# First batch's choice of an expert in single slots, early rows loaded in front of the early weights, first expert's rows loaded in two parts

## The chip, the core and the metric

The kernel runs on one core of a Trainium2 chip. The metric is the device time of one execution in microseconds (us). A core has TensorE (matrix products; PE in the profile), VectorE (DVE), ScalarE (ACT), GpSimd (POOL) and SyncE (SP, which here issues nearly all DMAs), each with an instruction queue of its own that it works through in order.

## The reference

Three stages: clustered attention, a layer of eight experts with one expert for each token, and a dense layer with a gate. 1536 tokens (2 batches of 768), 8 heads of 64, 512 channels.

```
mask   = q_assign == k_assign                      # cluster of each query and key: argmax over 16 centroids
attn   = softmax(where(mask, q k^T / 8, -1e9)) v   # per batch and head, 768 x 768
x      = attn as (1536, 512)
e_idx  = argmax(x w_gate); gate = softmax(x w_gate)[e_idx]; eom = sigmoid(x w_output_gate)[e_idx]
out[t] = gate * eom * relu(x[t] w1[e_idx]) w2[e_idx]          # w1 (8, 512, 1024), w2 (8, 1024, 512)
h      = out w_in;  result = (h * sigmoid(1.702 h)) w_out     # w_in (512, 2048), w_out (2048, 512), both 64-bit floats
```

## The kernel before

**Attention.** A unit is a batch and a pair of heads (8 units); a step is one head and 128 queries of a unit (96 steps, `steps`). In step i of the loop at L939 TensorE makes the scores of step i+1 (`emit_scores`), VectorE takes their maximum (L518), TensorE transposes the probabilities of step i-1 in two halves (`emit_pt`), the first of which ScalarE copies out (L537) and the second VectorE (L539), and ScalarE takes the exponential of step i+1 (L524). Products with v (L567) and with the output weights (L586) come in between, the latter into the only bank of the pool `ps_m`. The next unit's operands are prepared at fixed steps (`PLAN`): transposes, the split into high and low parts on GpSimd (L343, L344), stacks by DMA (L362), and the choice of clusters on VectorE (L391 to L405). Pieces of a conversion of the dense layer's 64-bit weights (`convert_early`, L125 to L135, written out at L176) run at fixed steps (`slots`).

**Routing.** As soon as a batch's attention, or half of the second batch's, is done, `route(gi)` chooses the experts of its tokens on VectorE (small instructions of 8 to 48 elements in each partition), counts, finds each token's row, scales the tokens, and scatters them to `xd` in memory (GpSimd, L730). It is a generator: `advance(2)` at L540 runs two pieces, from one `yield` to the next, after each half of a step's transposes, so a step has four slots. `route(0)` is put in at step 61. Its rank sums (L652 to L661) lie in a bank of `ps_m` that VectorE reads until L691. In the middle it picks the expert with the most tokens in the first batch (`soonh`, `soon`), and up to 128 of that expert's tokens (the early rows), which are computed during the rest of attention.

**Early rows.** `soon_at` sets the steps: at 75 `soon_ids` reads the expert and its row into registers of SyncE; at 84 seven loads of that expert's weights are issued, at 87 five more, and behind them the early rows (`soon_rows`, which waits for all scatters of the first batch); at 91 `soon_x` transposes the rows (L790). The products (`soon_products`, L806 and L816) run while the other groups are routed.

**Branch and experts.** Each expert has a capacity (`CAPS`, 304 for the first); if some expert has more tokens, a loop of surplus tiles runs inside `tc.If(trips > 0)` (L1233), which with these inputs is passed over. Every engine reads `trip` (L1228) and branches. Before that point two halves of the first expert's weights are loaded and split (`loads_to(2)`). Behind it `win_start(0, True)` loads the first expert's 304 rows in three pieces of 128, 128 and 48, each after all twelve scatters of L730; `loads_to(6)` loads four more halves of weights; `win_x` transposes the rows (L1118) and splits them (L1122, L1123); then the loop over 64 half blocks (L1337) and the dense layer (L1385 on) follow. Instructions are issued in the order in which they are written (`tc.manual_schedule`).

The lines on which the steps of the prediction rest:

```
921: soon_at = {75: [soon_ids], 84: [lambda: next(weights)], 87: [lambda: next(weights), soon_rows], 91: [soon_x]}
539:     nc.vector.tensor_copy(dst, src)
540: advance(2)
1102: for r0 in range(0, nr, 1 if pieces else nr):
1103:     m, p = (1, min(128, n - r0 * 128)) if pieces else (nr, 128)
```

Of the kernel before, what the change touches and what calls it, by code (L numbers as in the profile page):

```python
# [9 lines left out]
F32 = mybir.dt.float32  # L10
# [36 lines left out]
def attention_moe_ffn(ctx: ExitStack, tc: tile.TileContext, q, k, v, centroids, w_gate, w_og, w1, w2, w_in, w_out, out):  # L47
# [3 lines left out]
    def f32(ap):  # L51
        return ap.bitcast(F32)
# [553 lines left out]
    def route(gi):  # L606
# [62 lines left out]
        if gi == 0:  # L669
            nc.vector.scalar_tensor_tensor(lk, part, float(E), rev8, op0=ALU.mult, op1=ALU.add)  # L670
            lm, lv = new("lm", [128, 1]), new("lv", [128, E])
            nc.vector.tensor_reduce(lm, lk, op=ALU.max, axis=AX.X)
            nc.vector.tensor_scalar(soonh, lk, lm, None, op0=ALU.is_equal)
            yield
            nc.vector.tensor_tensor(lv, soonh, part, op=ALU.mult)
            nc.vector.tensor_reduce(ngone, lv, op=ALU.add, axis=AX.X)
            nc.vector.tensor_scalar(ngone, ngone, float(FIRST), None, op0=ALU.min)
            yield
            nc.vector.tensor_scalar(gone, soonh, ngone, None, op0=ALU.mult)
            nc.vector.scalar_tensor_tensor(sbase, gone, -1.0, ebase, op0=ALU.mult, op1=ALU.add)  # L680
            nc.vector.scalar_tensor_tensor(srev8, gone, -float(E), rev8, op0=ALU.mult, op1=ALU.add)
            yield
            nc.vector.tensor_tensor(lv, soonh, ebase, op=ALU.mult)
            nc.vector.tensor_reduce(span[:, 1:2], lv, op=ALU.add, axis=AX.X)
            nc.vector.tensor_tensor(span[:, 0:1], span[:, 1:2], ngone, op=ALU.subtract)
            yield
            nc.vector.tensor_tensor(lv, soonh, iota8, op=ALU.mult)
            nc.vector.tensor_reduce(lm, lv, op=ALU.add, axis=AX.X)
            nc.vector.tensor_copy(soon[:, 0:1], lm[0:1])
            nc.vector.tensor_copy(soon[:, 1:2], span[0:1, 0:1])  # L690
        nc.vector.tensor_tensor(dest, rk, sbase[:, None, :].to_broadcast([128, nj, E]), op=ALU.add)  # L691
# [229 lines left out]
    soon_at = {75: [soon_ids], 84: [lambda: next(weights)], 87: [lambda: next(weights), soon_rows], 91: [soon_x]}  # L921
# [173 lines left out]
    def win_load(ex_row, n, one_tile=False, pieces=False):  # L1095
        nr = -(-n // 128)
        if one_tile:
            x = hp.tile([128, 2 * CAP], F32R, name="ht", tag="ht")[:, None, :DM].bitcast(F32)
        else:
            x = xp.tile([128, WR, DM], F32, name="xr", tag="xr", bufs=1)  # L1100
        d = {"n": n, "nr": nr, "x": x}
        for r0 in range(0, nr, 1 if pieces else nr):
            m, p = (1, min(128, n - r0 * 128)) if pieces else (nr, 128)
            row = nc.s_assert_within(ex_row + r0 * 128, 0, E * NT - 128, skip_runtime_bounds_check_because="inside the rows of an expert") if r0 else ex_row
            x = nc.sync.dma_start(out=d["x"][:p, r0:r0 + m], in_=xd[bass.ds(row + FIRST, m * p)].rearrange("(r p) c -> p r c", p=p)).ins
            need(x, scatters)
        return d

    def win_x(d, r):
# [4 lines left out]
        m = min(128, d["n"] - r * 128)  # L1114
# [5 lines left out]
        hi = d["t"][:, :, n + r * 128:n + r * 128 + m]  # L1120
        src = pt.rearrange("p (k n) -> p k n", k=4)[:, :, :m]
        nc.scalar.copy(hi, src)  # L1122
        nc.vector.tensor_tensor(d["t"][:, :, r * 128:r * 128 + m], src, f32(hi), op=ALU.subtract)  # L1123
# [86 lines left out]
    hp = cx.enter_context(tc.tile_pool(name="hp", reuse_waits="tile", bufs=3))  # L1210

# [13 lines left out]
    some(100)  # L1225
    for f in low_parts:
        f()
# [94 lines left out]
    with tc.manual_schedule():  # L1322
        win_start(0, True)
# [169 lines left out]
```

## Time and profile before

| | us |
|---|---|
| median of 3 runs | 731.31 |
| lowest and highest | 730.92, 732.39 |
| profiled execution, its own time | 733.72 |
| span of the profiled execution | 732.0 |

| engine | busy us | share of the span |
|---|---|---|
| TensorE, products | 703.2 | 96% |
| VectorE | 458.1 | 63% |
| ScalarE | 393.0 | 54% |
| GpSimd | 264.4 | 36% |

A timeline has one line for each run of equal instructions of an engine: start, duration, engine, line of the kernel, operation, the tile written and those read, shapes, count, and in brackets how long the engine idled before it and who ended that. "issue" means that the engine waited for nothing that the profile shows; a name with q is an engine's sequencer. The table of stretches gives for each stretch its length, the busy time of each engine with its count of instructions, the mean granted clock of TensorE (1.00 is 2.4 GHz, 0.50 is 1.2 GHz), and the busy share and rate of the DMA engines. Attention takes the first 270 us, the branch lies near 280 us, the experts end near 460 us, and the dense layer takes the rest.

### The profile page before, as it was taken

To read this page: it belongs to the slowest core of one execution; us is meant where nothing else is said; L and a number is where in the kernel's file an instruction comes from. 1 tells how busy PE (TensorE), PEld (TensorE's weight loads), DVE (VectorE), ACT (ScalarE), POOL (GpSimd) and SP (SyncE) were. 2 spreads that over 40 slices of the span, in tenths; PEclk is the share of its full clock that TensorE was granted. 3 is DMA by queue.
4 is the path that set the end of the run, shared out by engine and by line. 5 is a ranking of instruction groups with operands and counts; after the bars stand their busy time and mean duration, and the time that the engine had idled before them with its cause. 6 is when DMAs were issued, how large, how long until landed. Compare 5 with 4: busy or idle time off the path is not lost.

```text
span 732.0 us, 12543 instructions
## 1 busy us (share of the span) xinstructions
PE 703.2 (96%) x4522; PEld 580.2 (79%) x4522; DVE 458.1 (63%) x886; ACT 393.0 (54%) x789; POOL 264.4 (36%) x219
## 2 busy tenths in 40 slices
PE   8999999998999898999999897999999999999996
PEld 6776776776866678999999887888888888888885
DVE  6969788889888774344554545687655657232322
ACT  7767675675666544556777676544534344222120
POOL 2230330312750013755978889222432212020202
PEclk8999999999899999999999999999999999999999
DMA  6778969637274427766477776132643211010101
GB/s 195 171 189 266 238 216 293 142 121 173 69 200 141 174 86 255 230 215 215 161 254 243 236 224 222 59 116 86 68 73 41 81 59 56 1 58 1 58 0 58
DMA packets 70594, 105.18 MB, mean 144 GB/s; under 512 B 9648, under 2 KB 48304, under 8 KB 70528
## 3 DMA queue, kind: packets, MB, share of 16 engines
q1 hardware_dynamic: 67584, 95.94, 45.9%
q0 software_dynamic: 2944, 8.40, 3.0%
q8 instruction: 37, 0.61, 0.4%
q14 instruction: 29, 0.24, 0.1%
HBM read 70.46 MB, written 14.69 MB: 116 GB/s over the span
## 4 chain that ended last, share of the span: by engine, by line
PE 33%; issue 16%; ACT 5%; DVE 3%; POOL 2%; DMA 1%; POOLq 0%; ACTq 0%; DVEq 0%
PE ph L1317 4%; PE ph L1318 4%; PE ph L1319 4%; PE py L1412 3%; PE py L1411 3%; PE py L1410 3%; PE py L1134 3%; ACT w L1048 3%; PE ph L1134 3%; PE ph L1135 1%; PE py L1135 1%; DVE w L1051 1%; DMA raw<-in_moe_w_dram 1%; POOL out_dram L1421 1%; ACT hs L1140 1%
## 5 line engine op out<-in xcount | busy, mean ns | idle before, releaser
L1051 POOL TENSOR_TENSOR w<-raw,w 128x1024 fp32r<-128x1024 f32 x51 | 125.6, 2482 | 39.3 <-ACT w L1048 38.9
L518 DVE TENSOR_REDUCE nm<-sp 128x1 f32<-128x768 f32 x96 | 91.6, 955 | 16.2 <-PE sp L516 14.1
L1395 DVE TENSOR_TENSOR sg<-ph,sg 128x512 f32<-128x512 f32 x48 | 33.2, 691 | 99.7 <-ACT sg L1394 97.5
L524 ACT ACTIVATE P<-sp,nm 128x768 f32<-128x768 f32 x96 | 87.2, 908 | 11.3 <-DVE nm L518 10.6
L532 PEld LDWEIGHTS pt<-ident,P 128*128 128x128 f32 x576 | 66.4, 143 | 28.1 <-issue 17.5
L532 PE MATMUL pt<-ident,P 128*128 128x128 f32 x576 | 84.3, 280 | 4.0 <-ACT pT L537 2.1
L1394 ACT ACTIVATE sg<-ph 128x512 f32<-128x512 f32 x48 | 28.7, 597 | 104.7 <-PE ph L1319 100.3
L1134 PE MATMUL py<-ht,w 128*128 128x512 f32 (+6 forms) x224 | 70.2, 367 | 8.0 <-DVE ht L1158 5.1
L515 PE MATMUL sp<-X,Q 128*128 128x384 f32 x192 | 74.9, 390 | 0.5 <-ACT P L524 0.4
L1412 PE MATMUL py<-w,gl 128*128 128x512 f32 (+1 forms) x194 | 75.2, 387 | 0.0
L1411 PE MATMUL py<-w,gh 128*128 128x512 f32 (+1 forms) x194 | 75.1, 387 | 0.0
L1410 PE MATMUL py<-w,gh 128*128 128x512 f32 (+1 forms) x194 | 75.0, 387 | 0.0
L1317 PE MATMUL ph<-yth,w 128*128 128x512 f32 x192 | 74.8, 390 | 0.0
L1318 PE MATMUL ph<-ytl,w 128*128 128x512 f32 x192 | 74.7, 389 | 0.0
L1319 PE MATMUL ph<-yth,w 128*128 128x512 f32 x192 | 74.7, 389 | 0.0
L1084 POOL TENSOR_TENSOR w<-csq,w 128x512 fp32r<-128x512 f32 x24 | 32.7, 1364 | 115.7 <-ACT w L1083 115.7
L1048 ACT CAST w<-raw 128x1024 fp32r<-128x1024 f32 x68 | 70.5, 1042 | 4.2 <-issue 2.4
L1134 PE MATMUL ph<-t,w 128*128 128x512 f32 (+6 forms) x224 | 69.4, 365 | 0.4 <-DVE ht L1158 0.4
L567 PE MATMUL po<-pT,ld_v 128*32 128x384 f32 x768 | 69.0, 492 | 0.0
L516 PE MATMUL sp<-Z,Q 80*128 80x384 f32 x192 | 66.4, 346 | 0.5 <-DMA Q<-ohT 0.5
L537 ACT COPY pT<-pt 128x384 f32<-128x384 f32 x96 | 45.8, 477 | 36.8 <-PE pt L532 36.8
L539 DVE COPY pT<-pt 128x384 f32<-128x384 f32 x96 | 52.8, 550 | 12.6 <-PE pt L532 12.2
(291 smaller groups left out, 1476.2 us busy)
## 6 DMA issues: line engine op xcount, KB each, us to landing
raw<-in_moe_w_dram SPq DMA_DIRECT2D x64, 512.0 KB, 4.5
raw<-in_moe_w_in_dram SPq DMA_DIRECT2D x16, 512.0 KB, 4.1
raw<-in_moe_w_out_dram SPq DMA_DIRECT2D x16, 512.0 KB, 4.8
xd<-zrow SPq DMA_DIRECT2D x8, 768.0 KB, 5.9
Q<-Hq SPq DMA_DIRECT2D x28, 192.0 KB, 2.7
ew<-in_moe_w_dram SPq DMA_DIRECT2D x9, 384.0 KB, 7.8
ld_q<-in_q_dram SPq DMA_DIRECT2D x8, 384.0 KB, 6.0
ld_k<-in_k_dram SPq DMA_DIRECT2D x8, 384.0 KB, 3.8
```

The costliest lines, as they stand in the source:

```text
L518: nc.vector.tensor_reduce(nm, sp[:, :, :384], op=ALU.max, axis=AX.XY, negate=True)
L524: nc.scalar.activation(P, L["sp"][:, :, :384], AF.Exp, bias=L["nm"], accum_out=L["sm"][:, h, j % 3:j % 3 + 1])
L532: nc.tensor.transpose(pt[:, r * 128:(r + 1) * 128], L["P"][:, n, r * 128:(r + 1) * 128], ident)
L1048: nc.scalar.copy(hi, r)
L1051: (eng or nc.gpsimd).tensor_tensor(lo, r, f32(hi), op=ALU.subtract)
L1134: nc.tensor.matmul(ps[:, :2 * n], w_hi, t, start=first, stop=False)
L1317: nc.tensor.matmul(ph, wa(key, 0, k, i), yth[:, k, cs], start=(k == 0), stop=False)
L1318: nc.tensor.matmul(ph, wa(key, 0, k, i), ytl[:, k, cs], start=False, stop=False)
L1319: nc.tensor.matmul(ph, wa(key, 1, k, i), yth[:, k, cs], start=False, stop=(k == 3))
L1410: nc.tensor.matmul(po[m][:, cs], gh[:, ms], wb(key, 0, i)[:, cs], start=first, stop=False)
L1411: nc.tensor.matmul(po[m][:, cs], gh[:, ms], wb(key, 1, i)[:, cs], start=False, stop=False)
L1412: nc.tensor.matmul(po[m][:, cs], gl[:, ms], wb(key, 0, i)[:, cs], start=False, stop=last)
```

## The change

1. In `route(0)`, the first batch's choice gets a `yield` after nearly every instruction. `dest` is started in the first slot from the rank sums and `ebase`, and `part` is copied to `c0`, so the bank isn't read after that; at the end of the choice `gone` is subtracted from `dest`.
2. In `soon_at`, `soon_rows` is called at step 84 in front of the first seven weight loads, and `soon_ids` at step 78.
3. `win_start(0, True)` is called in front of the reading of `trip` and the branch, and there loads only the first 128 rows, after the scatters of the first two groups; the last three scatters are declared to be without a dependency on it. Behind the branch `rest` loads the other 176 rows in one DMA of 88 partitions with two rows each, after all scatters. `win_x` then works on pieces of 128, 88 and 88 rows. The tile `xr` moves to a pool of its own, `xrp`, behind the pool `hp`.

```
--- before.py
+++ after.py
@@ -667,28 +667,44 @@
         if gi < len(GROUPS) - 1:
             lk = new("lk", [128, E])
         if gi == 0:
-            nc.vector.scalar_tensor_tensor(lk, part, float(E), rev8, op0=ALU.mult, op1=ALU.add)
-            lm, lv = new("lm", [128, 1]), new("lv", [128, E])
+            nc.vector.tensor_tensor(dest, rk, ebase[:, None, :].to_broadcast([128, nj, E]), op=ALU.add)
+            lm, lv, c0 = new("lm", [128, 1]), new("lv", [128, E]), new("c0", [128, E])
+            nc.vector.tensor_copy(c0, part)
+            yield
+            nc.vector.scalar_tensor_tensor(lk, c0, float(E), rev8, op0=ALU.mult, op1=ALU.add)
+            yield
             nc.vector.tensor_reduce(lm, lk, op=ALU.max, axis=AX.X)
+            yield
             nc.vector.tensor_scalar(soonh, lk, lm, None, op0=ALU.is_equal)
             yield
-            nc.vector.tensor_tensor(lv, soonh, part, op=ALU.mult)
+            nc.vector.tensor_tensor(lv, soonh, c0, op=ALU.mult)
+            yield
             nc.vector.tensor_reduce(ngone, lv, op=ALU.add, axis=AX.X)
+            yield
             nc.vector.tensor_scalar(ngone, ngone, float(FIRST), None, op0=ALU.min)
             yield
             nc.vector.tensor_scalar(gone, soonh, ngone, None, op0=ALU.mult)
+            yield
             nc.vector.scalar_tensor_tensor(sbase, gone, -1.0, ebase, op0=ALU.mult, op1=ALU.add)
+            yield
             nc.vector.scalar_tensor_tensor(srev8, gone, -float(E), rev8, op0=ALU.mult, op1=ALU.add)
             yield
             nc.vector.tensor_tensor(lv, soonh, ebase, op=ALU.mult)
+            yield
             nc.vector.tensor_reduce(span[:, 1:2], lv, op=ALU.add, axis=AX.X)
+            yield
             nc.vector.tensor_tensor(span[:, 0:1], span[:, 1:2], ngone, op=ALU.subtract)
             yield
+            nc.vector.tensor_copy(soon[:, 1:2], span[0:1, 0:1])
             nc.vector.tensor_tensor(lv, soonh, iota8, op=ALU.mult)
+            yield
             nc.vector.tensor_reduce(lm, lv, op=ALU.add, axis=AX.X)
+            yield
             nc.vector.tensor_copy(soon[:, 0:1], lm[0:1])
-            nc.vector.tensor_copy(soon[:, 1:2], span[0:1, 0:1])
-        nc.vector.tensor_tensor(dest, rk, sbase[:, None, :].to_broadcast([128, nj, E]), op=ALU.add)
+            yield
+            nc.vector.tensor_tensor(dest, dest, gone[:, None, :].to_broadcast([128, nj, E]), op=ALU.subtract)
+        else:
+            nc.vector.tensor_tensor(dest, rk, sbase[:, None, :].to_broadcast([128, nj, E]), op=ALU.add)
         if gi == len(GROUPS) - 2:
             nc.vector.scalar_tensor_tensor(lk, part, float(E), srev8, op0=ALU.mult, op1=ALU.add)
         yield
@@ -918,7 +934,7 @@
     slots.update({21: 3, 27: 1, 75: 1, 80: 1, 81: 2, 86: 3, 87: 2, 92: 2, 93: 2})
 
     weights = soon_weights()
-    soon_at = {75: [soon_ids], 84: [lambda: next(weights)], 87: [lambda: next(weights), soon_rows], 91: [soon_x]}
+    soon_at = {78: [soon_ids], 84: [soon_rows, lambda: next(weights)], 87: [lambda: next(weights)], 91: [soon_x]}
 
     fixed = ExitStack()
     fixed.enter_context(tc.manual_schedule())
@@ -1097,13 +1113,25 @@
         if one_tile:
             x = hp.tile([128, 2 * CAP], F32R, name="ht", tag="ht")[:, None, :DM].bitcast(F32)
         else:
-            x = xp.tile([128, WR, DM], F32, name="xr", tag="xr", bufs=1)
-        d = {"n": n, "nr": nr, "x": x}
-        for r0 in range(0, nr, 1 if pieces else nr):
-            m, p = (1, min(128, n - r0 * 128)) if pieces else (nr, 128)
+            x = xrp.tile([128, WR, DM], F32, name="xr", tag="xr")
+        d = {"n": n, "nr": nr, "x": x, "rows": [128] * (nr - 1) + [n - 128 * (nr - 1)]}
+
+        def rows_of(r0, m, p, names):
             row = nc.s_assert_within(ex_row + r0 * 128, 0, E * NT - 128, skip_runtime_bounds_check_because="inside the rows of an expert") if r0 else ex_row
             x = nc.sync.dma_start(out=d["x"][:p, r0:r0 + m], in_=xd[bass.ds(row + FIRST, m * p)].rearrange("(r p) c -> p r c", p=p)).ins
-            need(x, scatters)
+            for nm in scatters[len(names):]:
+                tc.declare_no_dep(x, nm, reason="an expert with 128 rows in these groups: later tokens have other rows")
+            need(x, names)
+
+        if pieces:
+
+            p = (n - 128) // (nr - 1)
+            d["rows"] = [128] + [p] * (nr - 1)
+            assert sum(d["rows"]) == n and LEAST >= 128
+            rows_of(0, 1, 128, scatters[:-GROUPS[-1][2]])
+            d["rest"] = lambda: rows_of(1, nr - 1, p, scatters)
+        else:
+            rows_of(0, nr, 128, scatters)
         return d
 
     def win_x(d, r):
@@ -1111,16 +1139,16 @@
 
             side = CAPS.index(d["n"]) % 2 if d["n"] in CAPS else 0
             d["t"] = xp.tile([128, 8 * CAPS[side]], F32R, name="t", tag=f"t{side}", bufs=1)[:, :8 * d["n"]].rearrange("p (k n) -> p k n", k=4)
-        m = min(128, d["n"] - r * 128)
+        m, r0 = d["rows"][r], sum(d["rows"][:r])
         xs = d["x"][:m, r]
         pt = bank("pxt")
         for k in range(4):
             nc.tensor.transpose(pt[:, k * 128:k * 128 + m], xs[:, k * 128:(k + 1) * 128], ident[:m, :m])
         n = d["n"]
-        hi = d["t"][:, :, n + r * 128:n + r * 128 + m]
+        hi = d["t"][:, :, n + r0:n + r0 + m]
         src = pt.rearrange("p (k n) -> p k n", k=4)[:, :, :m]
         nc.scalar.copy(hi, src)
-        nc.vector.tensor_tensor(d["t"][:, :, r * 128:r * 128 + m], src, f32(hi), op=ALU.subtract)
+        nc.vector.tensor_tensor(d["t"][:, :, r0:r0 + m], src, f32(hi), op=ALU.subtract)
 
     def product(ps, n, w_hi, w_lo, t, first, last):
 
@@ -1208,6 +1236,7 @@
 
     xp = cx.enter_context(tc.tile_pool(name="xp", reuse_waits="tile", bufs=2))
     hp = cx.enter_context(tc.tile_pool(name="hp", reuse_waits="tile", bufs=3))
+    xrp = cx.enter_context(tc.tile_pool(name="xrp", reuse_waits="tile", bufs=1))
 
     wins = {}
 
@@ -1223,6 +1252,7 @@
     relus[1]()
     low_parts.append(split_pair(ekeys[1], 0, None, nc.vector, True))
     some(100)
+    win_start(0, True)
     for f in low_parts:
         f()
     trips = nc.values_load_multi_w_load_instructions(trip, min_val=0, max_val=NOV)[1][0]
@@ -1320,7 +1350,7 @@
             ahead[g] = ph
 
     with tc.manual_schedule():
-        win_start(0, True)
+        wins[0]["rest"]()
         loads_to(6)
         banks.clear()
         banks.extend([(ps_m, "m"), (ps_t, "pt"), (ps_t, "pt"), (ps_a, "po")])
```

## Rows read from the trace of the kernel before

**Rows 1.** Table of stretches, core 0; busy us (x instructions) of each engine, granted clock.
```profile
core 0: us, PE busy (x) PEld busy (x) DVE busy (x) ACT busy (x) POOL busy (x), PEclk, DMA share, GB/s
177.71:192.44 14.73, 13.26 (x81) 10.46 (x85) 12.30 (x40) 6.98 (x15) 6.00 (x6) 0.77 0.13 48
212.80:223.10 10.30, 10.16 (x81) 7.96 (x85) 9.10 (x15) 7.04 (x15) 0.26 (x1) 1.00 0.55 156
181.00:187.00 6.00, 5.55 (x21) 5.00 (x21) 5.04 (x19) 2.37 (x5) 1.26 (x1) 0.50 0.00 0
249.00:253.00 4.00, 4.00 (x29) 2.43 (x31) 2.20 (x3) 2.29 (x5) 0.00 (x0) 0.61 0.00 0
283.90:288.80 4.90, 2.18 (x15) 1.46 (x14) 1.65 (x3) 2.22 (x4) 0.00 (x0) 1.00 0.97 300
289.70:293.10 3.40, 3.40 (x16) 3.40 (x15) 0.47 (x1) 2.15 (x3) 3.40 (x2) 0.50 0.93 295
```

**Rows 2.** Timeline of VectorE: start us, us, engine, line, operation, out<-in, [idle before].
```profile
177.71 0.95 DVE L518 TENSOR_REDUCE nm<-sp 128x1 f32<-128x768 f32 x1
178.58 0.19 DVE L664 TENSOR_REDUCE z<-zz 128x6 f32<-128x48 f32 x1
178.69 0.16 DVE L670 SCALAR_TENSOR_TENSOR lk<-prk,rev 128x8 f32<-128x8 f32 x1
178.88 0.16 DVE L672 TENSOR_REDUCE lm<-lk 128x1 f32<-128x8 f32 x1
...
179.80 0.55 DVE L539 COPY pT<-pt 128x384 f32<-128x384 f32 x1
...
182.62 0.18 DVE L691 TENSOR_TENSOR dest<-prk,sbase 128x48 f32<-128x48 f32 x1
```

**Rows 3.** Timeline of TensorE in the first batch's choice.
```profile
180.31 0.81 PE L532 MATMUL pt<-ident,P 128*128 128x128 f32 x3 [1.01 <-ACT pT L537]
...
182.86 1.97 PE L586 MATMUL pox<-wo,oa 128*128 128x160 f32 x6 [0.45 <-DVE dest L691]
```

**Rows 4.** Timeline of GpSimd; last, line 392's durations in ns (min/median/max, first and last start).
```profile
205.86 1.05 POOL L730 DMA_INDIRECT xd<-xs,di  x1 [0.28 <-POOL xs L725]
...
258.05 0.54 POOL L176 DMA_DIRECT2D wd<-zrow  x1 [17.89 <-DVE cnt L1232]
...
L392 DVE TENSOR_TENSOR eq<-sc,m x9: 357/558/1386, 10.6 to 207.6; 128x384 f32<-128x384 f32 x7, 128x192 f32<-128x192 f32 x2
```

**Rows 5.** Timeline of SyncE's issues: early weights, early rows.
```profile
229.19 4.61 SPq L760 DMA_DIRECT2D ew<-in_moe_w_dram  x7
...
239.66 0.34 SPq L782 DMA_DIRECT2D xs<-xd  x1
```

**Rows 6.** Timeline of TensorE: the early rows' transposes, the early weights' first products.
```profile
248.14 0.63 PE L790 MATMUL pxs<-ident,xs 128*128 128x128 f32 x4 [2.41 <-DMA xs<-xd]
...
267.35 0.94 PE L806 MATMUL pt<-xst,ew 128*128 128x128 f32 x6
```

**Rows 7.** Timeline of SyncE's issues on both sides of the branch.
```profile
268.86 0.96 SPq L1034 DMA_DIRECT2D raw<-in_moe_w_dram  x2
280.69 1.46 SPq L1105 DMA_DIRECT2D xr<-xd  x3
282.42 3.42 SPq L1034 DMA_DIRECT2D raw<-in_moe_w_dram  x4
```

**Rows 8.** Timeline of TensorE on both sides of the branch.
```profile
276.63 7.31 PE L816 MATMUL sp<-hsoon,ew 128*128 128x128 f32 x64
284.35 0.96 PE L1118 MATMUL pxt<-ident,xr 128*128 128x128 f32 x7 [0.40 <-PEq L1233]
286.74 0.70 PE L1118 MATMUL pxt<-ident,xr 128*128 128x128 f32 x5 [1.44 <-issue]
...
288.73 0.41 PE L1131 MATMUL ph<-t,w 128*128 128x304 f32 x1 [0.36 <-DVE t L1123]
```

**Rows 9.** Chain that ended last, in the loop over experts: start us, us, what.
```profile
408.14 8.21 DMA raw<-in_moe_w_dram
```

More of the change, by code (lines that the diff above doesn't have):

```diff
@@ L669, in route @@
         if gi == 0:
[L670 to L671 removed]
+            nc.vector.tensor_tensor(dest, rk, ebase[:, None, :].to_broadcast([128, nj, E]), op=ALU.add)
+            lm, lv, c0 = new("lm", [128, 1]), new("lv", [128, E]), new("c0", [128, E])
+            nc.vector.tensor_copy(c0, part)
+            yield
+            nc.vector.scalar_tensor_tensor(lk, c0, float(E), rev8, op0=ALU.mult, op1=ALU.add)
+            yield
             nc.vector.tensor_reduce(lm, lk, op=ALU.max, axis=AX.X)
+            yield
             nc.vector.tensor_scalar(soonh, lk, lm, None, op0=ALU.is_equal)
             yield
[L675 removed]
+            nc.vector.tensor_tensor(lv, soonh, c0, op=ALU.mult)
+            yield
             nc.vector.tensor_reduce(ngone, lv, op=ALU.add, axis=AX.X)
+            yield
             nc.vector.tensor_scalar(ngone, ngone, float(FIRST), None, op0=ALU.min)
@@ L920, in attention_moe_ffn @@
     weights = soon_weights()
-    soon_at = {75: [soon_ids], 84: [lambda: next(weights)], 87: [lambda: next(weights), soon_rows], 91: [soon_x]}
+    soon_at = {78: [soon_ids], 84: [soon_rows, lambda: next(weights)], 87: [lambda: next(weights)], 91: [soon_x]}
     fixed = ExitStack()
@@ L1099, in win_load, with rows_of @@
         else:
[L1100 to L1103, printed above, removed]
+            x = xrp.tile([128, WR, DM], F32, name="xr", tag="xr")
+        d = {"n": n, "nr": nr, "x": x, "rows": [128] * (nr - 1) + [n - 128 * (nr - 1)]}
+        def rows_of(r0, m, p, names):
             row = nc.s_assert_within(ex_row + r0 * 128, 0, E * NT - 128, skip_runtime_bounds_check_because="inside the rows of an expert") if r0 else ex_row
             x = nc.sync.dma_start(out=d["x"][:p, r0:r0 + m], in_=xd[bass.ds(row + FIRST, m * p)].rearrange("(r p) c -> p r c", p=p)).ins
-            need(x, scatters)
+            for nm in scatters[len(names):]:
+                tc.declare_no_dep(x, nm, reason="an expert with 128 rows in these groups: later tokens have other rows")
+            need(x, names)
+        if pieces:
+            p = (n - 128) // (nr - 1)
+            d["rows"] = [128] + [p] * (nr - 1)
+            assert sum(d["rows"]) == n and LEAST >= 128
+            rows_of(0, 1, 128, scatters[:-GROUPS[-1][2]])
+            d["rest"] = lambda: rows_of(1, nr - 1, p, scatters)
+        else:
+            rows_of(0, nr, 128, scatters)
         return d
@@ L1113, in win_x @@
             d["t"] = xp.tile([128, 8 * CAPS[side]], F32R, name="t", tag=f"t{side}", bufs=1)[:, :8 * d["n"]].rearrange("p (k n) -> p k n", k=4)
-        m = min(128, d["n"] - r * 128)
+        m, r0 = d["rows"][r], sum(d["rows"][:r])
         xs = d["x"][:m, r]
```

21 lines of the change are left out of this document (16 added, 5 removed).

## The prediction

> **What bounds the kernel now.** I read the page's busy shares first: TensorE is busy nearly throughout, so time is gained only where it idles or runs at the lower clock. The slices of granted clock on the page, and then the table of stretches, show three such places in the stretch that the change touches. Near 181 us the granted clock is 0.50 for six microseconds, which is the 1.2 GHz level; in 249 to 253 us it is 0.61 on average; and in 289.7 to 293.1 us it is 0.50 again [rows 1]. In front of each of them TensorE had idled. The timelines say on what.
>
> First place: TensorE waits for VectorE. In 180 to 183 us the transposes wait 1.01 us for ScalarE's copy and the output products wait 0.45 us for `dest` at L691 [rows 3], since `dest` is the last reader of the bank that `route` holds. VectorE runs the first batch's choice there in groups of three and more small instructions [rows 2]. Five attention steps, counted from one maximum at L518 to the fifth after it, take 14.73 us there; the same five steps of the next unit, with the same 81 matmuls, take 10.30 us [rows 1].
>
> Second place: the transposes of the early rows (L790) wait 2.41 us for `xs` [rows 6]. SyncE issued that load at 239.66 us, behind twelve loads of early weights that began at 229.19 us [rows 5]; the weights' first product runs at 267.35 us [rows 6].
>
> Third place: behind the branch. TensorE ends the early products at 283.94 us (276.63 + 7.31), goes through the branch in 0.40 us, does seven of the twelve row transposes at once, and then stands 1.44 us with the releaser "issue" [rows 8], that is, on nothing that the profile shows. The first product of the first expert that goes on without pause starts at 288.73 us [rows 8].
>
> **The choice in single slots.** Nothing of the arithmetic goes; two instructions come (the copy `c0` of `part`, the later subtraction from `dest`). `advance(2)` runs two slots after each half of a step, four in a step. Before, `route(0)` takes five slots from its rank sums to the end of `dest`; after, it takes seventeen, so the small work spreads over four and a quarter steps and scatters start three steps later (12 slots).
>
> VectorE was busy 12.30 us of the 14.73 with 40 instructions, and 9.10 us of the usual 10.30 with 15 [rows 1]. So 25 small instructions cost 3.20 us, 0.128 each. By slots, 26 of them will lie in the same five steps: 9.10 + 26 x 0.128 = 12.4 us if VectorE never idles. That is 2.3 us less than 14.73: the idle time of VectorE, in which it waited for a TensorE at half clock. I allow 0.3 us of idle and take 2.0 us. The bank `prk` is free after the first slot instead of at `dest`, so the 0.45 us wait goes, inside this sum.
>
> The lower bound is 0.3 us: the first stall of 1.01 us is in the same step as before, and if the granted clock falls all the same, three of the five steps stay bound by TensorE at half speed. The upper bound is 3.1 us. A chained pair (L670 to L672) starts 0.19 us apart, an unchained one (L664 to L670) 0.11 [rows 2]; some ten chained ones would each lose 0.08 us if the next big instruction (reduction, copy) lies between. The Trainium skill speaks against this last part: "VectorE: DVE Perf Modes", section "Rules for kernel authors", says of chained operations to minimize their count and not their semaphores, since the pipe drains after each anyway. By it the spread saves nothing by itself, and the two added instructions cost 0.26 us; the rows disagree with it by 0.08 us an instruction, and I leave that part out of the sum for another reason, that two slots in a row still chain.
>
> What follows the choice is GpSimd's scattering, six tiles of rows that end with the issue at 205.86 us [rows 4]. Three steps later means up to 10.7 us later (at the long steps' 3.6 us), 216.6 us. Behind them in GpSimd's queue lie the splits of unit 7's keys, which move in between the scatters and not behind all of them; they are due with the unit's stacks, which its first scores read a unit of steps later. They take another time beside VectorE, though: one L392 took 1386 ns where the median is 558 [rows 4]. The Trainium skill, "SBUF — State Buffer", section "SBUF: two separate sides", gives a reason: GpSimd and a VectorE instruction with two inputs in SBUF exclude each other for the whole of one. By that the scatters' scalings, now under that stage, could stop VectorE three times. I take 0, as the collision only changes its partner; the bounds are 0.8 us of gain (none collides) and 0.8 us of loss (two do).
>
> **Early rows in front of weights.** `soon_rows` moves ahead of the seven and five weight loads; `soon_ids` moves from step 75 to 78, with nothing of SyncE's due between. The scatters that the load waits for have ended by 216.6 us on the old clock, 12 us ahead of the 229.19 at which it is now issued; behind it on SyncE's queue stand the twelve weight loads, with 38 us to their first use [rows 5, 6], so the added issue is hidden, and would cost some 0.4 us without that cover. The rows need what the load needed behind twelve others, at most 8.5 us (239.66 to 248.14), and are awaited 16 us after. So the 2.41 us go. The next thing due is the transposes of probabilities, ready by then. The lower clock behind the gap goes as well: 0.61 over 4.00 us is 3.1 us at half speed with TensorE busy throughout [rows 1], worth 1.56 us. Together 4.0 us; bounds 2.4 (the clock falls anyway) and 4.2.
>
> **Rows of the first expert.** The first 128 rows' load moves ahead of the reading of `trip` and the branch. Its condition is the scatters of the first two groups; on SyncE's queue it stands behind the two weight loads of 268.86 us, and behind it stand only that reading and the branch. The other 176 rows come in one load of 88 partitions, two rows each, instead of two. SyncE issued three row loads in 1.46 us from 280.69 us, then the weights from 282.42 us [rows 7]; two issues fewer bring the weights 1.0 us forward. But TensorE's seven transposes ran at 284.35 us without a wait, the stall behind them names no load, and the first weights behind the branch are not what TensorE waits for at 288.73 [rows 8]. So I take 0. Against: rows 128 and on now land only when all 176 are there; without the stall as cover that is up to 0.9 us. For: if the 1.44 us are a consequence of the traffic (DMA share 0.97 in that stretch) they may shrink, and the half clock of 3.40 us that follows, worth 1.7 us, may go [rows 1]: at best 3.1 us.
>
> **Sum.** 2.0 + 4.0 + 0 = 6.0 us. The profiled span of 732.0 us becomes 726.0; the profiled execution's own time of 733.72 us lies 1.7 above its span and 2.4 above the median of the runs shown, so I carry the gain over: 731.31 - 6.0 = 725.3 us. What follows the branch moves as a whole, since the loads of the loop over experts are released by its own splits.
>
> **The rivals.**
> (1) The choice keeps its cost: granted clock stays at 0.50 there, and GpSimd's scalings stop VectorE. Gain 4.0 + 0.3 - 0.8 = 3.5 us: 727.8. For it: VectorE stays fully busy over five steps.
> (2) The stall behind the branch goes too: 6.0 + 3.1 = 9.1 us, 722.2. For it only the DMA share; against it "issue".
> (3) The gain is eaten in the loop over experts, where one weight load is awaited for 8.21 us [rows 9]: if a shifted overlap of transfers lengthens two such waits by half, 8 us would go; by a quarter of one, 2: 727.3. Against it: order and sizes of these loads stay.
> (4) Slower: the load ahead of the branch holds SyncE. `xr` gets a pool behind `hp`, over the room of the conversion tiles; GpSimd's last write-out of those starts at 258.05 us [rows 4], so it should be free. If instead it were free only at the last early product (283.94), SyncE's row load for the others would slide from 280.69 to some 286.5, and the first product from 288.73 by as much or by 7 us with the lower clock: 725.3 + 7 = 732.3, slower than before. It decides from the point where SyncE is freed 6 us after 278 us.
> (5) The change doesn't do what it says: scatters later than 229 us would hold SyncE and all weights. The 12 us of room speak against, and then the weights have 38 us of their own: no loss below that.
>
> **How the numbers follow.** The forecast, with gains of 4.5 to 7.5 us, has 0.62; rival 1 has 0.16, rival 2 has 0.10, rival 3 has 0.07 (half of it near no change), rival 4 has 0.04, and 0.01 is left for others. The range goes from rival 2 to just past rival 1: 721.9 to 728.5 us. A measurement of this kernel can tell about 0.2%, 1.5 us, from no change; faster by more than that 0.91, within it 0.05, slower 0.04.
>
> **What would show it.** In the profile after, the choice: granted clock 1.00 through its steps, five steps in some 12.7 us, no wait of the output products for `dest`. Early rows: no idle of TensorE at L790, its load issued ahead of the first weight load, clock 1.00 behind. Branch: a row load issued before the branch, one after it, and the wait named "issue" still there. Wrong would be: a wait of SyncE in front of either moved load, scatters that end after step 84, a loop over experts that takes longer than before, or a gain at the branch above 1 us.

## The result and the profile after

| | before | after |
|---|---|---|
| median, us | 732.39 (5 runs, 730.92 to 733.12) | 726.10 (5 runs, 724.77 to 728.17) |
| ratio of the times, 95% interval | | 0.992 [0.9895, 0.9945] |
| profiled execution, own time / span, us | 733.72 / 732.0 | 728.17 / 726.5 |

The kernel is faster by 5.9 us (4.0 to 7.7, the ratio times 732.4); 6.0 were forecast. In a second series the same kernel took 726.55 us (ratio 0.9922 [0.9897, 0.9947]). The profiled execution was the longest of its five, which matters below.

**The choice.** Table of stretches of the kernel after: five steps from one maximum at L518 to the fifth after it, as in [rows 1], then the next five, then eight (columns as there: length, busy us and count of PE, PEld, DVE, ACT, POOL, granted clock, DMA share, GB/s).

```profile
177.99:189.90 11.91, 11.02 (x89) 8.11 (x93) 11.60 (x42) 7.68 (x17) 0.00 (x1) 1.00 0.07 25
189.90:200.38 10.48, 10.48 (x88) 9.17 (x84) 9.37 (x18) 8.46 (x20) 6.96 (x7) 1.00 0.14 44
200.38:222.62 22.24, 21.75 (x193) 14.48 (x186) 18.71 (x32) 13.30 (x29) 15.65 (x15) 1.00 0.76 204
```

The same three in the kernel before:

```profile
177.71:192.44 14.73, 13.26 (x81) 10.46 (x85) 12.30 (x40) 6.98 (x15) 6.00 (x6) 0.77 0.13 48
192.44:203.70 11.26, 11.26 (x96) 9.42 (x92) 9.65 (x15) 9.23 (x22) 10.11 (x10) 1.00 0.31 103
203.70:226.69 22.99, 21.91 (x193) 14.50 (x186) 19.41 (x32) 13.31 (x29) 7.04 (x8) 1.00 0.58 153
```

The eighteen steps take 44.63 us in place of 48.98: 2.82 us less in the first five, 0.78 in the next five, 0.75 in the last eight, and the granted clock stays at 1.00. Eight of TensorE's products lie in the first five steps now and not in the next five (89 and 88 in place of 81 and 96), so these ten are best read together. VectorE's timeline shows single small instructions between the large ones, and the last scatter's issue on GpSimd lies at 215.94 us:

```profile
179.08 0.15 DVE L672 COPY c<-prk 128x8 f32<-128x8 f32 x1
179.26 0.17 DVE L674 SCALAR_TENSOR_TENSOR lk<-c,rev 128x8 f32<-128x8 f32 x1
179.35 0.55 DVE L539 COPY pT<-pt 128x384 f32<-128x384 f32 x1
179.81 0.15 DVE L676 TENSOR_REDUCE lm<-lk 128x1 f32<-128x8 f32 x1
...
215.94 1.02 POOL L746 DMA_INDIRECT xd<-xs,di  x1 [0.28 <-POOL xs L741]
```

**Early rows.** SyncE's issues, and TensorE's transposes of the early rows (now L806), of the kernel after:

```profile
221.18 2.07 SPq L435 DMA_DIRECT2D Q<-ohT  x2
...
226.25 0.38 SPq L798 DMA_DIRECT2D xs<-xd  x1
226.83 4.35 SPq L776 DMA_DIRECT2D ew<-in_moe_w_dram  x7
...
242.02 0.60 PE L806 MATMUL pxs<-ident,xs 128*128 128x128 f32 x4
```

The load stands in front of the weights, and the wait of 2.41 us at the transposes [rows 6] is gone, as is the half clock behind it. One new wait is there, ahead of it, in the scores of step 84:

```profile
223.98 0.44 PE L516 MATMUL sp<-Z,Q 80*128 80x384 f32 x1 [0.60 <-DMA Q<-ohT]
```

**Branch.** TensorE around it, a row of the table of stretches behind it, and SyncE's issues (after). The transposes of the rows are L1146, the products L1158 to L1160.

```profile
276.62 0.63 PE L1146 MATMUL pxt<-ident,xr 128*128 128x128 f32 x4 [0.41 <-PEq L1263]
277.79 0.45 PE L1146 MATMUL pxt<-ident,xr 88*128 88x88 f32 x3 [0.54 <-DMA xr<-xd]
280.99 0.60 PE L1146 MATMUL pxt<-ident,xr 88*128 88x88 f32 x5 [2.76 <-issue]
282.18 0.62 PE L1158 MATMUL ph<-t,w 128*128 128x304 f32 x1 [0.59 <-ACT t L1150]
...
282.20:288.80 6.60, 6.59 (x25) 6.25 (x26) 1.03 (x3) 3.17 (x4) 5.65 (x3) 0.50 0.79 277
...
270.14 4.01 SPq L1121 DMA_DIRECT2D xr<-xd  x2
274.48 2.25 SPq L1050 DMA_DIRECT2D raw<-in_moe_w_dram  x4
```

Against [rows 8] the gap named "issue" is 2.76 us in place of 1.44, the rows are awaited for 0.54, and the half clock that follows lasts 6.8 us (granted clock 0.50 over 282.2 to 288.8) in place of 3.4. From the end of the early products to the first product it takes 5.97 us, 4.02 before. Counted from TensorE's first instruction, the end of the early products is 7.7 us earlier than before, the first product 5.8, and from the 24th product to the end it stays at 4.8 to 5.5: nothing is lost in the loop over experts.

So the trace reads as two errors that cancel: a choice worth twice its forecast, and a branch that costs some 2 to 3 us where 0 was forecast. The experiments were made on this reading, and it held only in part.

### The profile page after: what moved, and what is told of

Its sections match the earlier page's. It is cut to its first block, busy times and chain, and to the rows that moved or that the text cites. A ratio compares the mean times of both kernels' runs of the same rounds, so it can differ in the third digit from the quotient of the medians.

```text
span 726.5 us, 12540 instructions
## 1 busy us (share of the span) xinstructions
PE 700.6 (96%) x4522; PEld 578.9 (80%) x4522; DVE 457.4 (63%) x888; ACT 392.4 (54%) x789; POOL 263.0 (36%) x219
## 4 chain that ended last, share of the span: by engine, by line
PE 33%; issue 16%; ACT 5%; DVE 3%; POOL 2%; DMA 2%; POOLq 0%; ACTq 0%; SPq 0%; DVEq 0%
PE ph L1347 4%; PE ph L1349 4%; PE ph L1348 4%; ACT w L1064 3%; PE py L1442 3%; PE py L1440 3%; PE py L1441 3%; PE py L1162 3%; PE ph L1162 2%; PE py L1163 1%; DVE w L1067 1%; PE ph L1163 1%; POOL out_dram L1451 1%; DVE ph L1169 1%; ACT hs L1168 1%
## 5 line engine op out<-in xcount | busy, mean ns | idle before, releaser
L518 DVE TENSOR_REDUCE nm<-sp 128x1 f32<-128x768 f32 x96 | 91.6, 955 | 14.2 <-PE sp L516 13.0
L515 PE MATMUL sp<-X,Q 128*128 128x384 f32 x192 | 73.4, 382 | 0.4 <-ACT P L524 0.4
```

Of the source, the lines that this page charges most:

```text
L518: nc.vector.tensor_reduce(nm, sp[:, :, :384], op=ALU.max, axis=AX.XY, negate=True)
```

## The experiments

The theory: each of the first two parts gains by itself what the trace shows, and the third loses at the branch. The rivals: the third is free and one of the others gives less; or the longer gap comes from the traffic of the loads, from the shape of the second row load, or from chance. Times are compared by the ratio to the kernel before on the same chip, whose medians lay between 732.1 and 732.7 us.

**Choice alone**: the first part of the diff on the kernel before, and nothing else.

> The kernel before with the first part alone (the choice in single slots). Theory A, from the two traces: the first maxima (L518, numbered from 0) show where time went; between maximum 60 and maximum 83 the kernel after gained 4.35 us (0.28 late at 60, 4.07 early at 83), all of it the choice's. So 4.3 us at the early rows, and about 727.5 to 728.5 us at a before of 732. The stall behind the branch stays near the 1.44 us of before. Rival B (the parts have no price of their own, the moments at which the clock falls decide): the granted clock falls once more in the choice or in front of the branch, and the gain is under 2 us.

Measured: 729.06 us, ratio 0.9961 [0.9944, 0.9978], a gain of 2.9 us (1.6 to 4.1). Its trace has the stretches of the changed kernel (11.92 and 10.48 us). That is less than the 4.35 us between the two traces above, and its interval takes in the forecast 2.0; neither of the two expectations (4.3 us, or under 2) came. The next kernel shows why.

**Early rows alone**:

```diff
-    soon_at = {75: [soon_ids], 84: [lambda: next(weights)], 87: [lambda: next(weights), soon_rows], 91: [soon_x]}
+    soon_at = {78: [soon_ids], 84: [soon_rows, lambda: next(weights)], 87: [lambda: next(weights)], 91: [soon_x]}
```

> The kernel before with the second part alone (early rows in front of the weights). Theory A: maxima 92 to 95 gain 4.2 us, some 0.5 us may be lost at step 84 behind the loads: 3.7 to 4.2 us, about 728 us at a before of 732. Stall behind the branch near 1.44 us. Rival B: under 2 us, as the lower clock only comes elsewhere.

Measured: 727.53 us, ratio 0.9949 [0.9929, 0.9968], a gain of 3.7 us (2.3 to 5.2). This kernel has the old choice, and its trace (table of stretches, the ten steps of the choice) is what corrects the reading of the first part:

```profile
177.74:191.06 13.32, 10.56 (x81) 7.79 (x85) 12.29 (x41) 6.97 (x15) 4.67 (x5) 1.00 0.12 45
191.06:202.25 11.19, 11.19 (x96) 9.44 (x92) 10.02 (x15) 9.17 (x22) 10.09 (x9) 1.00 0.26 88
```

The same 81 products, the same busy time of VectorE, and a granted clock of 1.00: the old choice takes 13.32 us when the clock doesn't fall, and 14.73 when it does. Whether it falls differs between executions of the same code.

**The two parts together**, rows of the first expert as before:

> The kernel after without its third part: the first expert's rows in three loads behind the branch, as before. Theory A: all 7.7 us that the kernel after had gained at the end of the early products reach the end, since the branch costs what it cost before (stall 1.44 us with the releaser issue, no wait for rows, one stretch of half clock): 724 us at a before of 732, some 2.5 us less than the kernel after. Rival B: the longer stall behind the branch (2.76 us after 0.54 us for rows) and the longer half clock come from the shift in time and not from part three; then it is there here too, and the time is the kernel after's, 726.

Measured: 725.01 us, ratio 0.9905 [0.9887, 0.9923]. The product of the two single ratios is 0.9910, so the gains add up. The expected distance of 2.5 us to the changed kernel isn't there: by the ratios, from two chips, it is 1.1 us, and the intervals overlap.

**First expert's rows alone**: `win_load`, `win_x`, the pool `xrp` and the two calls, on the kernel before.

> The kernel before with the third part alone (128 rows loaded ahead of the branch, 176 behind it). Theory A: no gain at the rows, SyncE held in front of the branch until the first rows have landed (0.85 us in the kernel after), TensorE waiting about 0.5 us for rows and over 2 us with the releaser issue: 2 to 3 us slower than before, 734 to 735 us at 732. Rival B: as before, within 1 us. A third, that of the recorded forecast: 0 with 0.9 us of loss to 3.1 of gain.

Measured: 734.09 us, ratio 1.0003 [0.9984, 1.0023]: by the ratio no difference (from 1.2 us faster to 1.7 slower). Its median, though, lies 2.0 us above that of the kernel before on the same chip (732.08 us), as theory A expected, so this run alone doesn't decide between the two. Its trace has the long gap again (2.71 us, rows awaited 0.37), and the granted clock is 1.00 in its old choice too, five steps in 13.33 us:

```profile
177.13:190.46 13.33, 10.55 (x81) 7.79 (x85) 12.28 (x40) 6.98 (x15) 4.67 (x5) 1.00 0.12 45
```

**The other rows in two loads** of 128 and 48, behind the branch:

```diff
-            p = (n - 128) // (nr - 1)
-            d["rows"] = [128] + [p] * (nr - 1)
+            d["rows"] = [128] * (nr - 1) + [n - 128 * (nr - 1)]
...
-            d["rest"] = lambda: rows_of(1, nr - 1, p, scatters)
+            def rest():
+                for r0 in range(1, nr):
+                    rows_of(r0, 1, d["rows"][r0], scatters)
+            d["rest"] = rest
```

> The kernel after, with the 176 rows behind the branch in two loads of 128 and 48 rows as before (the first 128 still ahead of the branch). Theory S (shape: the load of 88 partitions with two rows each lands late, TensorE stands on it and the stall named issue begins later): no wait for rows on TensorE, the stall back from 2.76 us to 1.4 to 1.6 us, some 1.5 us less than the kernel after. Theory P (place: a load in flight when SyncE comes to the branch, whose landing it awaits there, 0.85 us): SyncE's wait stays, the loads behind stay late, wait for rows and longer stall stay; time of the kernel after.

Measured: 726.36 us, ratio 0.99 [0.9861, 0.9939]. TensorE behind the branch:

```profile
278.16 0.95 PE L1149 MATMUL pxt<-ident,xr 128*128 128x128 f32 x7 [0.41 <-PEq L1266]
281.39 0.96 PE L1149 MATMUL pxt<-ident,xr 128*128 128x128 f32 x5 [2.28 <-issue]
```

The wait for the rows is gone, as theory S expected, and the gap stays, against it.

**All rows behind the branch**, the others still in one load:

```diff
-            rows_of(0, 1, 128, scatters[:-GROUPS[-1][2]])
+            rows_of(0, 1, 128, scatters)
...
-    win_start(0, True)
     for f in low_parts:
...
+        win_start(0, True)
         wins[0]["rest"]()
```

> The kernel after, with both row loads (128, then 176 in one) behind the branch. Theory P: SyncE passes the branch without its wait, the row loads are issued 0.5 us earlier against the early products' end than in the kernel after, no wait for rows or under 0.3 us, stall 1.4 to 1.6 us: the time of the two parts without the third, 725 us at 732. Theory S: wait for rows 0.5 us or more and stall over 2.5 us stay, 726 us.

Measured: 725.39 us, ratio 0.9903 [0.9871, 0.9935].

```profile
278.51 0.63 PE L1146 MATMUL pxt<-ident,xr 128*128 128x128 f32 x4 [0.40 <-PEq L1262]
279.81 0.45 PE L1146 MATMUL pxt<-ident,xr 88*128 88x88 f32 x3 [0.68 <-DMA xr<-xd]
281.73 0.60 PE L1146 MATMUL pxt<-ident,xr 88*128 88x88 f32 x5 [1.47 <-issue]
```

The wait for the rows thus goes with the single load of 176 rows and not with the place of the first load: with the single load it was seen in four executions of five (0.37 to 0.68 us), without it in none. The gap was 1.47 us here; at that point I took the longer one to come from the load ahead of the branch.

**Fewer weights behind the branch**: the two parts, and two halves of weights fewer in front of the transposes.

```diff
-        loads_to(6)
+        loads_to(4)
```

> The two parts without the third, with two of the four weight loads behind the branch issued later (1 MB less beside the rows). Theory T (the stall named issue is instruction code that waits behind transfers): the stall falls from 1.55 us to about 1.0 to 1.2 us. Rival: it is the fetch's own duration, 1.4 to 1.6 us as before. If the loop over experts then waits for these weights, some tenths are lost there.

Measured: 727.51 us, ratio 0.9936 [0.9916, 0.9956]. The gap is 0.99 us. In the kernel with the two parts it was 1.28 (not the 1.55 of the expectation), but 0.98 in a second execution of it further down, so an effect of the loads on the gap isn't shown. TensorE pays later, where it waits for the low part of the early rows' result inside the loop; the 50th product is 4.5 us earlier than before, where it is 9.0 with the two parts:

```profile
290.67 0.62 PE L1146 MATMUL py<-ht,w 128*128 128x304 f32 x1 [2.87 <-DVE ytl L1372]
```

**Gap filled**: the two parts, and sixteen products of the identity with itself, without use, between the last transpose and the first product.

```diff
         for r in range(wins[0]["nr"]):
             win_x(wins[0], r)
+        keep_clock_last(16)
```

> The two parts without the third, with 16 short products without use (128 columns, bf16) behind the first expert's row transposes on TensorE, while ScalarE and VectorE split the rows. Theory: TensorE's idle time there (0.5 us and 0.4 us) is filled at no cost and the stretch of half clock behind it goes, 1.0 to 1.7 us less: 723.5 us at 732. Rival: the stall named issue in front is enough for the lower clock, and the filling costs up to 0.3 us: 725 to 725.5 us.

Measured: 723.78 us, ratio 0.9891 [0.9864, 0.9918], the fastest so far. There is no half clock behind the branch.

**Four kernels once more, on one chip.** Single traces had carried the reading of the branch, so the changed kernel, the two parts and the filled gap ran again side by side, with the changed kernel with its gap filled (the same line, on the kernel after).

> The changed kernel once more, on one chip with the three kernels that follow, so that they can be compared with one another. If moving the first expert's rows costs what the trace shows at the first product behind the branch (3.2 us against the kernel with the two other parts alone, and up to 4.2 us at the 24th product), its median lies 2 to 5 us above that kernel's. If the trace of one execution misleads and the rows' move is free in the mean, the two medians lie within 1 us of one another. The stall named issue on TensorE behind the branch again 2.3 to 2.9 us, the wait for xr 0.4 to 0.7 us.

> The choice in single slots and the early rows in front, the rows of the first expert as before. If their move costs, 2 to 5 us below the changed kernel on this chip (some 722 to 724 us where that takes 726); if it is free, equal to it. The stall named issue 1.2 to 1.5 us and no wait for xr.

> The changed kernel with sixteen products without use on TensorE between the last transpose of the rows and the first product. If only the half clock made the rows' move dear, they take it away and the time comes to within 1 us of the filled kernel without that move, 723 to 724 us. If the longer stall (2.8 us) and the wait for the 176 rows (0.5 us) stay, the first product comes 1.5 to 2.5 us later than there, and if TensorE has gone to the lower clock within the stall already, sixteen small products come too late: granted clock 0.50 behind them for some 5 us, time as the changed kernel's or up to 1 us above it.

> The choice in single slots, the early rows in front, rows of the first expert as before, sixteen products without use between the transposes and the first product. By the first look 1 to 2 us below the kernel without them (the 24th product 1.9 us earlier); no half clock behind the branch. If that came from the chance of one execution, equal to it.

| | median, us (runs) | ratio to before | gap "issue", us |
|---|---|---|---|
| changed kernel | 726.55 (6) | 0.9922 [0.9897, 0.9947] | 0.92 |
| the two parts | 726.31 (6) | 0.9920 [0.9894, 0.9946] | 0.98 |
| changed kernel, gap filled | 725.14 (6) | 0.9901 [0.9874, 0.9929] | 2.49 |
| the two parts, gap filled | 723.45 (5) | 0.9882 [0.9855, 0.9909] | 1.71 |

TensorE behind the branch in the changed kernel's second execution:

```profile
277.56 0.63 PE L1146 MATMUL pxt<-ident,xr 128*128 128x128 f32 x4 [0.47 <-PEq L1263]
278.71 0.45 PE L1146 MATMUL pxt<-ident,xr 88*128 88x88 f32 x3 [0.53 <-DMA xr<-xd]
280.08 0.60 PE L1146 MATMUL pxt<-ident,xr 88*128 88x88 f32 x5 [0.92 <-issue]
281.27 0.41 PE L1158 MATMUL ph<-t,w 128*128 128x304 f32 x1 [0.59 <-ACT t L1150]
```

My theory of a steady loss falls: 2 to 5 us between the first two kernels were expected, and 0.2 came out. The same program had a gap of 2.76 us in one execution and 0.92 in the other. The wait for the rows is the same (0.54 and 0.53).

What ends the gap shows in the DMA view. Its row for the queue of instructions (queue, kind: packets, MB, share of 16 engines) has one packet of 16 KB near the branch. For the changed kernel's first execution, in 278.3 to 279.5 us, and for its second, in 277.5 to 278.8 us:

```profile
q8 instruction: 1, 0.02, 5.7%
...
q8 instruction: 1, 0.02, 5.8%
```

Worked out from the packets' times in every trace, counted from the first transpose of the rows:

| execution | packet starts | took | ends | eighth transpose |
|---|---|---|---|---|
| first rows ahead of the branch | | | | |
| after, first / second execution | 1.74 / -0.03 | 1.10 / 1.22 | 2.83 / 1.18 | 4.37 / 2.52 |
| after, gap filled | 0.99 | 1.08 | 2.06 | 3.48 |
| first rows alone | 1.70 | 1.09 | 2.79 | 4.16 |
| others in two loads | -0.40 | 2.42 | 2.02 | 3.24 |
| no row load ahead | | | | |
| before | -0.57 | 1.68 | 1.11 | 2.40 |
| choice alone | -0.64 | 1.09 | 0.45 | 1.91 |
| early rows alone | -0.58 | 1.18 | 0.59 | 1.95 |
| two parts, first / second | 0.01 / -0.52 | 0.94 / 0.94 | 0.95 / 0.42 | 2.23 / 1.94 |
| all rows behind | 0.96 | 1.12 | 2.08 | 3.22 |
| fewer weights | -0.44 | 1.01 | 0.57 | 1.95 |
| gap filled, first / second | -0.30 / 0.11 | 1.09 / 1.62 | 0.79 / 1.74 | 2.18 / 2.67 |

In all fourteen executions the transposes go on 0.9 to 1.5 us after that packet has ended, whatever else is different. So the gap ends after the arrival of instructions, and its length follows from when the packet starts and how long it takes among the loads. (The trace doesn't name the engine that a packet is for, but it tells: between the last five packets of this queue, which start from 600.3 to 715.8 us in the kernel after, lie 252 to 257 of TensorE's weight loads and products each time, and one or none of SyncE's instructions. So the queue brings TensorE's instructions. That one packet ends the gap rests on the order in time.) The Trainium skill, "Runtime: NRT & Kernel Launch", section "Instruction fetch mechanics", has the rule: instructions come in blocks of 16 KiB, and a taken branch to a block that isn't held stops the engine until that block is fetched. The trace agrees in the size of the packet and in an engine that stands until one has landed, and "issue" in [rows 8] is read as this; but TensorE had already done seven transposes behind the branch each time, so it stood behind the branch's target and not at it. With the row load ahead the packet ends after 2.2 us in the mean of five, without it after 1.0 in the mean of nine; the two groups overlap (1.18 to 2.83, 0.42 to 2.08), so the load may make a late packet likelier, but five executions don't settle it.

The filled gap does hold: in both series it is the fastest, and in its two traces the products behind the branch run 0.14 us apart from the third on. Without it they run 0.25 us apart for a while in ten of eleven traces. The eleventh is that of the early rows alone, where nothing was filled and the granted clock stayed at 1.00 behind a gap of 0.99 us, while it fell with the choice alone behind one of 0.95. Table of stretches, 6.6 us from the first product on, early rows alone and choice alone:

```profile
281.37:287.97 6.60, 6.24 (x42) 6.02 (x43) 2.32 (x6) 5.56 (x8) 5.54 (x3) 1.00 1.01 350
282.29:288.89 6.60, 6.24 (x31) 6.02 (x32) 1.19 (x3) 4.04 (x6) 5.62 (x3) 0.74 0.87 284
```

So two traces without half clock are a hint for the filling, and not a proof. After the changed kernel's long gap the sixteen products come too late (gap 2.49, 0.25 us apart all the same for a dozen products). Second execution of the two parts with the gap filled, TensorE:

```profile
279.76 0.70 PE L1134 MATMUL pxt<-ident,xr 128*128 128x128 f32 x5 [1.71 <-issue]
280.40 1.07 PE L219 MATMUL sp<-identb 128*128 128x128 bf16 x16
281.28 0.38 PE L1146 MATMUL ph<-t,w 128*128 128x304 f32 x1
...
282.00 0.30 PE L1148 MATMUL ph<-t,w 128*128 128x304 f32 x1
282.14 0.30 PE L1146 MATMUL ph<-t,w 128*128 128x304 f32 x1
```

Against the kernel with the two parts it gains 1.0 us by the first pair of ratios (0.9905 and 0.9891, two chips) and 2.9 us on the chip that ran both; the intervals overlap both times, so its size is open, and its sign was the same twice. Beside the changed kernel it is 3.1 us faster on that chip, and the slowest of its five runs (724.53) is faster than the quickest of the changed kernel's six (724.92).

## Why the prediction was right

The time was right (725.3 forecast, 726.1 and 726.55 measured), and the sum of the single parts by their ratios is 2.9 + 3.7 - 0.2 = 6.4 us, against 2.0 + 4.0 + 0. That the total came out to a few tenths of a us is in part luck: the choice gained for another reason than the one given, and a loss at steps 83 to 85 that wasn't foreseen is too small to show in the times. By steps:

**Choice: 2.0 us forecast, 2.9 (1.6 to 4.1) measured. The size was about right, and the reason was wrong.** The step read 25 small instructions at 0.128 us, let 26 of them cost 12.4 us with VectorE never idle, and put the whole gain down to the idle time behind a TensorE at half clock. But the old choice without half clock takes 13.32 us, so of the 14.73 the clock was 1.41, and it fell in one of three traces with the old choice. The five steps then take 11.91 us, not 12.7. The idle time is as allowed: 11.91 - 11.60 = 0.31. What was mis-sized is the instruction: 27 more than in [rows 1]'s usual steps cost 11.60 - 9.10 = 2.50 us, 0.093 each. The 0.8 us of chained starts, which the rows showed [rows 2] and which I left out, are there: by 0.128 the 27 would have cost 3.46 us. The Trainium skill, "VectorE: DVE Perf Modes", section "Rules for kernel authors", which says that the count matters and not the chaining, would have had the two added instructions cost 0.26 us and the spread save nothing; here the measurement decides against it: 42 instructions took 11.60 us where 40 had taken 12.30, and 12.28 where no half clock lay over them.

Over ten steps the undisturbed old choice takes 13.32 + 11.19 = 24.51 us and the new one 22.39: 2.1 us. That is nearest to the 2.9 of the time; the rest of the 4.35 in the two traces above is the half clock of that one execution and, in part, one stretched instruction, which the prediction took for a collision: L392, 1386 ns at the most before [rows 4], took at the most 682 ns after and 558 in the kernel with the early rows alone, whose scatters lie as before. So it wasn't a property of the old order either, and no run shows what stretched it. The forecast's zero for it, with 0.8 us on both sides, was a fair price. The upper bound of 3.1 us was not: an execution of before with the half clock loses 4.35 us to the new one.

**Early rows: 4.0 us forecast, 3.7 (2.3 to 5.2) measured.** From the maximum of step 92 to that of step 95 the trace loses 4.2 us in every kernel that has this part, and the granted clock stays at 1.00 there. Unlike at the choice, the half clock behind the late rows was there in all three traces that have them (before, choice alone, first rows alone).

One cost was missing in the sum, a small one: none was set for what SyncE issues ahead of the moved row load ("with nothing of SyncE's due between"). In all ten traces that have both of the first two parts, one of SyncE's eight issues of the stacks at step 83 is stretched from 0.58 us to between 0.98 and 1.52, and it ends 0.37 us after an instruction packet of 16 KB has landed (in the kernel after, the packet takes 0.97 us until 222.25, inside the issue pair of 221.18 us above). In the four others the packet starts 0.5 us or more before the first of these issues, and none is stretched. The scores wait for the last stacks in all but the shortest case: the two steps from the maximum of step 83 to that of 85 take 3.15 to 4.45 us (mean 3.88) in place of 3.11. That is 0.8 us in the mean, and 0.5 in the kernel after. The same section of the Trainium skill says that crossing from one block to the next in straight code is mostly hidden; in these ten traces it showed, at another engine: by the count above the packets of this queue are TensorE's and not SyncE's own. The early rows alone have the same moves of `soon_ids` and `soon_rows` and no stretched issue, so these don't do it by themselves. Why the packet comes later with both parts, and how it holds SyncE's issue, stays open; no run moved it by itself.

**Rows of the first expert: 0 forecast, -0.2 (-1.7 to 1.2) measured alone; beside the kernel without it a loss of 0.2 us on one chip (726.55 and 726.31), and of 1.1 by the first pair of ratios (0.992 and 0.9905).** The forecast holds in the time, and its mechanism in parts: the added wait is there as priced (0.54 us of the 0.9 at most), and the stall named "issue" is still there, and ends with no load of the rows. The trace of the longest execution made it look like a loss of 2 to 3 us; the second execution of the same program has 4.18 us from the early products to the first product in place of 5.97, and the kernel with the two parts 3.86 and 3.57. With the gap filled the two kernels differ by 1.7 us (725.14 and 723.45, intervals overlapping). The medians of the kernel with the third part alone and of the kernel before differ by 2.0 us. So a cost of 0 to 2 us is left open: the wait of 0.5 us for the single load is shown, a packet that comes later more often is not.

SyncE did wait in front of the moved load, which I had named as a sign of error: 5.3 us for the scatters of the second group, until 270.14 us. It cost nothing, since only the reading of `trip` stood behind it. At the branch itself SyncE was held for 0.85 us while the row load was under way. This is a wait of the program: the instruction at which it stood names the semaphore of that load (108), and SyncE passed 0.02 us after its last update, in four traces of four; where the load had landed before, the same step took 0.07 us. SyncE had both row loads issued by 274.15 us (270.14 + 4.01), 2.1 us before the early products' end at 276.2.

**The rivals.** Rival 1 (choice keeps its cost) and rival 2 (the stall goes too) didn't come. Rival 3 is excluded by the constant distance through the loop, rival 4 by SyncE's free passage: the load for the other rows was issued right behind the branch. The last scatter came at 215.94 us, as worked out (216.6), and rival 5 with it was off.

## What to carry to other kernels

Half clock behind a gap of TensorE can come and go between executions of the same code: before a gain is put down to it, look at a second trace with the same code, as the kernels with one part alone gave here for nothing. A gap with the releaser "issue" behind a branch is to be read against the queue of instructions in the DMA view; a few products without use behind such a gap gained more here (1.0 to 2.9 us, its size open) than moving the loads around it. Chained small instructions on VectorE got cheaper by being put singly between large ones (0.093 us in place of 0.128), even with two more of them.

## What the runs showed of the hardware

- The queue with the 16 KB instruction packets is TensorE's: 252 to 257 of its weight loads and products lie between two of the last five packets, with one or none of SyncE's instructions. Behind the branch TensorE went on 0.9 to 1.5 us after the end of such a packet, in 14 of 14 executions; that packet took 0.94 to 2.42 us among the loads, and the gap varied from 0.92 to 2.76 us for the same program.
- The same kind of packet (0.97 us in the kernel after) lay under a stretched DMA issue of SyncE (0.58 us usual, 0.98 to 1.52), with no branch near, in ten executions of ten with both first parts; the issue ended 0.37 us after the packet.
- With a row load under way, the program's wait for that load's semaphore held SyncE at the branch for 0.37 to 0.85 us, in four executions; the same step took 0.07 us in the ten others.
- 176 rows in one load of 88 partitions with two rows each were awaited 0.37 to 0.68 us in four executions of five; as two loads of 128 and 48 rows they were not awaited in any.
- The granted clock fell to 0.50 under the old choice in one of three traces, behind a wait of 1.01 us [rows 3] that is in the two traces without the fall too (1.01 and 1.00). Behind the branch it fell after an unfilled gap of 0.95 us and stayed at 1.00 after one of 0.99.
